# Layer-norm factors of an S4 and SwiGLU kernel: mean times scale factor on GpSimd in place of VectorE

## Chip, cores and metric

One core of a Trainium2 chip runs the whole program. The metric is the device time of one execution in microseconds (us). The program before was timed three times: median 1091.86 us, lowest 1090.23, highest 1092.86.

## What is computed

Two layers of the same pair of blocks work on `x` with 2048 rows of 512 features. In the reference:

```python
x = A_u
x = x + _A_ref(_layernorm(x, axis=-1), ...)   # S4: long convolution of each feature
x = x + _B_ref(_layernorm(x, axis=-1), ...)   # SwiGLU: (silu(x @ w_gate) * (x @ w_up)) @ w_down
x = x + _A_ref(_layernorm(x, axis=-1), ...)
x = x + _B_ref(_layernorm(x, axis=-1), ...)

def _layernorm(x, axis=-1, eps=1e-5):
    m = jnp.mean(x, axis=axis, keepdims=True)
    v = jnp.var(x, axis=axis, keepdims=True)
    return (x - m) / jnp.sqrt(v + eps)
```

The inner width of `_B_ref` is 1376. `_A_ref` builds a convolution kernel of 2048 taps for each of the 512 features from 128 complex modes and convolves along the rows.

## The kernel before

The rows are cut into four blocks of 512 rows (`T`, `NB`). Up to about 330 us the program builds the convolution kernels and their spectra, splits the weights into two fp16 halves, and does the first block's convolution; three norms of that part use another function, `stats`, which the diff does not touch. From then on it runs the steady part: for each pair of layer and block, in the order `SEQ = ((0, 0), (0, 1), (0, 2), (1, 0), (0, 3), (1, 1), (1, 2), (1, 3))`, the convolution of the next pair stands beside the feed-forward part of the present one.

- The convolution of a pair (`ssm_half`, two halves of 256 features). `inputs` loads the block into `n` (L238), `norm_x` normalises it in place (L255, four groups of 128 rows), `forward` splits it into two fp16 parts `z` (ScalarE L267, VectorE L232 in the helper `stt`) and transforms it on TensorE (L277); ScalarE (L278) and VectorE (L232, L285, L292) make spectra of it, and GpSimd stores them in DRAM (L739). VectorE multiplies spectra with those of the convolution kernel and adds up over earlier blocks (L812, L815; loads L808 and L810 on the SP queue), combines (L820, L821, L767, L768, L833 to L845), and the inverse transform runs on TensorE (L784) from an fp16 split `yl` (ScalarE L776, VectorE L232). The result is added into the block's rows (L793, or L232 with `pi`).
- The feed-forward part (`ffn`), twice per pair with 256 rows each. `ffn_norm` normalises two groups of 128 rows: L883 on ScalarE, then the fp16 split L884 (ScalarE) and L885 (VectorE), then the transposes L887 by DMA on the SP queue. `remainder` (L899 to L901, L906 to L913) takes the last 96 of the 1376 columns, the lines L930 to L939 the others: matrix products, silu on ScalarE (L936), product on VectorE (L937), fp16 split (ScalarE L938, VectorE L939). The product with `w_down` (L946 to L948) is added to the rows on VectorE (L953) and stored (L957).

Both norms of the steady part take their factors from `row_stats`, which is what the change edits. It returns `rs`, the reciprocal standard deviation, and `nb`, minus the mean times `rs`. Sums come from the accumulator of ScalarE's activation: L223 a scaled sum, L225 a sum of squares around the mean, L226 one operation on 2 or 4 columns that adds epsilon. GpSimd raises to the power -0.5 (L227), VectorE multiplies (L228), and ScalarE's L255 or L883 reads both as `scale` and `bias`. The feed-forward norms ask for `scale` = 256, the convolution's for 1.

`norm_x` runs 6 times (four columns) and `ffn_norm` 15 times (two columns); the first feed-forward half has its norm from the earlier part. The junk output of the sums goes to a scratch tile.

Each engine works through its own list in order. The lists of the early part are laid down by hand (`manual_schedule`). In the steady part a planner sets the order when the program is built: it replays the program with its own costs and due times (`schedule_with_timeline_sim=True`) and prefers what stands under `tc.high_priority(offset=BOOST)`, which holds for `ffn_norm`, the split lines of `ffn` and the transforms. An operation that waits for another engine holds up whatever stands behind it in its list.

Of the kernel before, what the change touches and what calls it, by code (L numbers as in the profile page):

```python
# [15 lines left out]
AF = mybir.ActivationFunctionType  # L16
OP = mybir.AluOpType
# [4 lines left out]
L, D, F = 2048, 512, 1376  # L22
# [53 lines left out]
def kernel(ctx, tc, x, a_re, a_im, b_re, b_im, c_re, c_im, log_dt, d_skip,  # L76
                           w_gate, w_up, w_down, c_ef, c_ei, c_ek, c_am, c_eh, c_eih, out):
    nc = tc.nc
    V, A, G, PE = nc.vector, nc.scalar, nc.gpsimd, nc.tensor
# [9 lines left out]
    def tl(shape, name, tag, dt=F32):  # L89
        return sb.tile(shape, dt, name=name, tag=tag, bufs=BUFS[tag])  # L90
# [50 lines left out]
    epst = sb.tile([P, 2], F32, name="epst")  # L141
# [74 lines left out]
    def row_stats(src, rows, scale, tag, junk):  # L216

        mv = tl([P, 4, 2], "mv", tag)
        rs = tl([P, 8], "rs", tag)
        nb = rs[:, 4:]  # L220
        c = 1.0 / (math.sqrt(D) * scale)
        for r in range(rows):
            A.activation(junk(r), src[:, r], AF.Identity, scale=-c / D, accum_out=mv[:, r, 0:1])  # L223
        for r in range(rows):
            A.activation(junk(r), src[:, r], AF.Square, scale=c, bias=mv[:, r, 0:1], accum_out=mv[:, r, 1:2])  # L225
        A.activation(mv[:, :rows, 1], mv[:, :rows, 1], AF.Identity, bias=epst[:, 0:1] if scale == 1.0 else epst[:, 1:2])  # L226
        G.tensor_tensor(rs[:, :rows], mv[:, :rows, 1], mhalf[:, :rows], OP.pow)  # L227
        V.scalar_tensor_tensor(nb[:, :rows], mv[:, :rows, 0], 1.0 / c, rs[:, :rows], OP.mult, OP.mult)  # L228
        return rs, nb

    def stt(o, i0, s, i1, op1):
# [20 lines left out]
    def norm_x(n):  # L252
        rs, nb = row_stats(n, 4, 1.0, "stats", lambda r: tl([P, D], "junk", "t1", BF16))
        for c in range(4):
            A.activation(n[:, c], n[:, c], AF.Identity, scale=rs[:, c:c + 1], bias=nb[:, c:c + 1])  # L255
# [618 lines left out]
    def ffn_norm(layer, b, s):  # L874

        rows = TB // P
        xt = xs[SEQ.index((layer, b)) % 3][:, s * rows:(s + 1) * rows]
        nh, nlo = nhl2[:, s % 2, 0], nhl2[:, s % 2, 1]
        with tc.high_priority(offset=BOOST):
            rs, nb = row_stats(xt, rows, 256.0, "stats2", lambda r: nn2[:, r])  # L880
            nt = nn2[:, 1].bitcast(F16).rearrange("p (i k) -> p i k", i=2)
            for r in range(rows):
                A.activation(nn2[:, 0], xt[:, r], AF.Identity, scale=rs[:, r:r + 1], bias=nb[:, r:r + 1])  # L883
                A.activation(nt[:, 0], nn2[:, 0], AF.Copy)  # L884
                V.tensor_tensor(nt[:, 1], nn2[:, 0], nt[:, 0], OP.subtract)  # L885
                for i, o in enumerate((nh, nlo)):
                    nc.sync.dma_start_transpose(o[:, :, r * P:(r + 1) * P], nt[:, i])  # L887
        return nh, nlo
# [86 lines left out]
    with tc.manual_schedule(engines={mybir.EngineType.Activation, mybir.EngineType.DVE, mybir.EngineType.PE, mybir.EngineType.Pool}):  # L975
# [170 lines left out]
        c, kts = NCH - 1, (kt2[:, 0], kt2[:, 1])  # L1146
# [160 lines left out]
```

## Time and profile before

| | |
|---|---|
| median of three runs | 1091.86 us |
| the profiled execution, time | 1091.58 us |
| the profiled execution, span from first to last instruction | 1089.4 us |
| granted TensorE clock, mean | 0.986 |
| busy: TensorE, VectorE, ScalarE, GpSimd | 1026.5, 969.3, 547.4, 109.6 us |

In the rows of the trace PE is TensorE (PEld its weight loads), DVE VectorE, ACT ScalarE, POOL GpSimd, and SP the queue that issues most transfers; a `q` behind an engine's name is its sequencer. L227 is line 227 of the program. A row of the timeline begins with start and duration in us, then engine, line, operation, written and read tiles, shapes and count; in brackets stands the idle time of the engine in front of it and what ended it. A row of the waits has the waiting operation, the one it waited for, the total in us, the number of times, and the longest. Matrix operations are pipelined and their ends are modelled; spans on GpSimd are rough.

### The profile page before, as it was taken

To read this page: it belongs to the slowest core of one execution; us is meant where nothing else is said; L and a number is where in the kernel's file an instruction comes from. 1 tells how busy PE (TensorE), PEld (TensorE's weight loads), DVE (VectorE), ACT (ScalarE), POOL (GpSimd) and SP (SyncE) were. 2 spreads that over 40 slices of the span, in tenths; PEclk is the share of its full clock that TensorE was granted. 3 is DMA by queue.
4 is the path that set the end of the run, shared out by engine and by line. 5 is a ranking of instruction groups with operands and counts; after the bars stand their busy time and mean duration, and the time that the engine had idled before them with its cause. 6 is when DMAs were issued, how large, how long until landed. Compare 5 with 4: busy or idle time off the path is not lost.

```text
span 1089.4 us, 22811 instructions
## 1 busy us (share of the span) xinstructions
PE 1026.5 (94%) x9302; PEld 810.9 (74%) x9302; DVE 969.3 (89%) x1405; ACT 547.4 (50%) x1093; POOL 109.6 (10%) x163
## 2 busy tenths in 40 slices
PE   1989999998779999999999999999999999999998
PEld 1868888887677777686779676786867687686775
DVE  8999999998999999999999989999998999993221
ACT  6989998953367162466462253533425432134211
POOL 1112222220002010012010001201100000000000
PEclk9989999998989999999999999999999999999999
DMA  5366777768765356342444553443545245312000
GB/s 212 108 180 167 173 166 179 187 181 272 234 182 172 120 145 215 105 141 68 131 117 133 158 160 130 119 136 100 166 126 180 59 127 147 109 61 63 2 25 20
DMA packets 125003, 149.23 MB, mean 137 GB/s; under 512 B 50897, under 2 KB 75985, under 8 KB 124130
## 3 DMA queue, kind: packets, MB, share of 16 engines
q1 hardware_dynamic: 112994, 122.27, 36.8%
q0 software_dynamic: 11904, 25.50, 10.0%
q8 instruction: 73, 1.20, 0.5%
q14 instruction: 32, 0.26, 0.1%
HBM read 97.66 MB, written 33.82 MB: 121 GB/s over the span
## 4 chain that ended last, share of the span: by engine, by line
PE 27%; DVE 27%; issue 11%; DMA 5%; ACT 3%; POOL 1%; SPq 0%; DVEq 0%; POOLq 0%; ACTq 0%
PE pgu L930 5%; PE pgu L931 5%; PE pgu L933 5%; DVE t L812 4%; DVE yk L815 4%; PE py L948 3%; PE py L946 3%; PE py L947 3%; DVE yk L812 3%; PE pi L784 2%; DVE sg L937 2%; DVE hl L939 2%; DMA n<-xdr 1%; DVE yl L232 1%; DMA mix<-nn 1%
## 5 line engine op out<-in xcount | busy, mean ns | idle before, releaser
L930 PE MATMUL pgu<-mix,wsl 128*128 128x256 f16 x1280 | 298.6, 273 | 5.4 <-DVE sg L937 2.1
L931 PE MATMUL pgu<-mix,wsl 128*128 128x256 f16 x1280 | 298.4, 273 | 0.0
L933 PE MATMUL pgu<-mix,wsl 128*128 128x256 f16 x1280 | 194.8, 273 | 0.0
L931 PEld LDWEIGHTS <-wsl 128*128 128x128 f16 x1280 | 125.2, 98 | 22.5 <-issue 6.7
L933 PEld LDWEIGHTS <-wsl 128*128 128x128 f16 x1280 | 125.2, 98 | 18.4 <-issue 3.8
L930 PEld LDWEIGHTS <-wsl 128*128 128x128 f16 x1280 | 125.2, 98 | 16.4 <-issue 1.2
L946 PE MATMUL py<-wsl,hh 128*128 128x512 f16 (+1 forms) x352 | 134.2, 381 | 0.1
L948 PE MATMUL py<-wsl,hl 128*128 128x512 f16 (+1 forms) x352 | 133.5, 381 | 0.1
L947 PE MATMUL py<-wsl,hh 128*128 128x512 f16 x320 | 121.8, 381 | 0.0
L815 DVE TENSOR_TENSOR yk<-yk,t 128x1024 f32<-128x1024 f32 x96 | 116.9, 1218 | 0.5
L812 DVE TENSOR_TENSOR t<-uu,w 128x1024 f32<-128x1024 f32 x96 | 117.0, 1218 | 0.3
L938 ACT ACTIVATE hh<-sg 128x512 f16<-128x512 f32 x80 | 50.1, 627 | 114.0 <-DVE sg L937 114.0
L544 PE MATMUL pw<-kt,ek 128*128 128x256 f32 (+1 forms) x384 | 93.2, 381 | 0.0
L937 DVE SCALAR_TENSOR_TENSOR sg<-pgu,sc,sg 128x512 f32<-128x512 f32 x80 | 59.6, 745 | 37.7 <-ACT sg L936 37.6
L936 ACT ACTIVATE sg<-pgu,sc 128x512 f32<-128x512 f32 x80 | 54.2, 678 | 70.7 <-PE pgu L933 66.9
L544 PEld LDWEIGHTS pw<-kt,ek 128*128 128x128 f32 x384 | 74.8, 199 | 8.8
L939 DVE TENSOR_TENSOR hl<-sg,hh 128x512 f16<-128x512 f32 x80 | 54.8, 685 | 15.3 <-ACT hh L938 15.3
L227 POOL TENSOR_TENSOR rs<-mv,mhalf 128x2 f32<-128x2 f32 (+1 forms) x21 | 33.6, 1598 | 336.3 <-ACT mv L226 296.3
L509 PE MATMUL pk<-re,g 128*32 128x64 f32 x1024 | 65.0, 317 | 2.2 <-DMA g<-g 1.9
L948 PEld LDWEIGHTS <-hl 128*128 128x128 f16 (+1 forms) x352 | 34.4, 98 | 39.2 <-issue 0.8
L947 PEld LDWEIGHTS <-hh 128*128 128x128 f16 (+1 forms) x352 | 34.6, 98 | 38.4 <-issue 0.8
L510 PE MATMUL pk<-im,g 128*32 128x64 f32 x1024 | 63.1, 301 | 0.0
(265 smaller groups left out, 2010.1 us busy)
## 6 DMA issues: line engine op xcount, KB each, us to landing
uu<-udr SPq DMA_DIRECT2D x96, 256.0 KB, 3.0
w<-wdr SPq DMA_DIRECT2D x96, 256.0 KB, 2.8
g<-g POOLq DMA_DIRECT2D x6, 1024.0 KB, 9.2
udr<-fu POOLq DMA_DIRECT2D x22, 256.0 KB, 2.7
udr<-u SPq DMA_DIRECT2D x16, 256.0 KB, 3.3
n<-xdr SPq DMA_DIRECT2D x4, 1024.0 KB, 6.4
kdr<-ks SPq DMA_DIRECT2D x6, 512.0 KB, 2.9
kt<-kdr SPq DMA_DIRECT2D x24, 128.0 KB, 3.0
```

Source lines behind the costliest of these rows:

```text
L509: PE.matmul(o, lhsT=g[:, 0, :, d], rhs=re[:, 0:64, d], start=True, stop=False, tile_position=(0, 32 * grp))
L544: PE.matmul(pw[:, i], lhsT=e, rhs=kt[:, :, c + 4 * k0:4 * k1:4, :].rearrange("p g k d -> p k g d"), start=c == 0, stop=c == 3)
L812: V.tensor_tensor(t, uu.unsqueeze(2).to_broadcast([P, NQ, 2, 2, DC]), w.unsqueeze(3).to_broadcast([P, NQ, 2, 2, DC]), OP.mult)
L815: V.tensor_tensor(yk, yk, t, OP.add)
L930: PE.matmul(o, lhsT=wgu(wi, k, 0)[:, fs], rhs=nh[:, k], start=k == 0, stop=False)
L931: PE.matmul(o, lhsT=wgu(wi, k, 1)[:, fs], rhs=nh[:, k], start=False, stop=False)
L933: PE.matmul(o, lhsT=wgu(wi, k, 0)[:, fs], rhs=nlo[:, k], start=False, stop=k == 3)
L937: V.scalar_tensor_tensor(sg, pgu[:, 1], sc6[:, 4:5], sg, OP.mult, OP.mult)
L939: V.tensor_tensor(hl[:, f0:f0 + 2], sg, hh[:, f0:f0 + 2], OP.subtract)
L946: PE.matmul(py[r], lhsT=hh[:n, f, rc], rhs=wd(f, 0)[:n], start=f == 0, stop=False)
L947: PE.matmul(py[r], lhsT=hh[:n, f, rc], rhs=wd(f, 1)[:n], start=False, stop=False)
L948: PE.matmul(py[r], lhsT=hl[:n, f, rc], rhs=wd(f, 0)[:n], start=False, stop=f == FT - 1)
```

## The change

The sums are no longer scaled: L223 yields minus the mean itself, L225 the plain sum of squares around it, and the constant 1 / (512 x scale^2) moves into L226. With the mean unscaled, its product with `rs` needs no constant, so it is a plain product of two small tiles, and it is issued on GpSimd behind the power instead of on VectorE. ScalarE's readers then wait for GpSimd instead of VectorE. `stats` stays as it is.

```diff
         mv = tl([P, 4, 2], "mv", tag)
         rs = tl([P, 8], "rs", tag)
         nb = rs[:, 4:]
-        c = 1.0 / (math.sqrt(D) * scale)
+        c = 1.0 / (D * scale ** 2)
         for r in range(rows):
-            A.activation(junk(r), src[:, r], AF.Identity, scale=-c / D, accum_out=mv[:, r, 0:1])
+            A.activation(junk(r), src[:, r], AF.Identity, scale=-1.0 / D, accum_out=mv[:, r, 0:1])
         for r in range(rows):
-            A.activation(junk(r), src[:, r], AF.Square, scale=c, bias=mv[:, r, 0:1], accum_out=mv[:, r, 1:2])
-        A.activation(mv[:, :rows, 1], mv[:, :rows, 1], AF.Identity, bias=epst[:, 0:1] if scale == 1.0 else epst[:, 1:2])
+            A.activation(junk(r), src[:, r], AF.Square, bias=mv[:, r, 0:1], accum_out=mv[:, r, 1:2])
+        A.activation(mv[:, :rows, 1], mv[:, :rows, 1], AF.Identity, scale=c,
+                     bias=epst[:, 0:1] if scale == 1.0 else epst[:, 1:2])
         G.tensor_tensor(rs[:, :rows], mv[:, :rows, 1], mhalf[:, :rows], OP.pow)
-        V.scalar_tensor_tensor(nb[:, :rows], mv[:, :rows, 0], 1.0 / c, rs[:, :rows], OP.mult, OP.mult)
+        G.tensor_tensor(nb[:, :rows], mv[:, :rows, 0], rs[:, :rows], OP.mult)
         return rs, nb
```

## Prediction

> **What bounds the kernel now.** First the page: busy time, and the chain that ended last.
>
> ```profile
> span 1089.4 us, 22811 instructions
> PE 1026.5 (94%) x9302; PEld 810.9 (74%) x9302; DVE 969.3 (89%) x1405; ACT 547.4 (50%) x1093; POOL 109.6 (10%) x163
> ...
> PE 27%; DVE 27%; issue 11%; DMA 5%; ACT 3%; POOL 1%; SPq 0%; DVEq 0%; POOLq 0%; ACTq 0%
> ```
>
> TensorE and VectorE share the chain; GpSimd is idle nine tenths of the time but still holds 1% of the chain. The changed function first runs at 331 us. Second, the windows view, for the stage in which VectorE still convolves and for the one in which only feed-forward work is left.
>
> ```profile
> 330.00:870.00 540.00, 527.51 (x4404) 401.19 (x4402) 521.90 (x786) 245.22 (x481) 51.60 (x62) 1.00 0.45 133
> 900.00:1060.00 160.00, 160.00 (x1347) 120.93 (x1346) 98.66 (x140) 43.13 (x77) 2.00 (x5) 1.00 0.24 68
> ```
>
> Columns: length, then busy time of PE, weight load, DVE, ACT, POOL. From 900 on TensorE has no idle time: nothing saved there on another engine can count. Between 330 and 870 TensorE is idle 540 - 527.5 = 12.5 us and VectorE 540 - 521.9 = 18.1 us. So 12.5 us is the most that a change of the norms can win, and ScalarE, busy 45%, matters only where something queued on it is late. Third, the waits of 330 to 870, VectorE's and then TensorE's.
>
> ```profile
> DVE hl L939 <- ACT hh L938: 7.0, 4, 3.0
> DVE rs L228 <- POOL rs L227: 5.0, 8, 1.2
> ...
> PE pi L784 <- ACT yl L776: 5.8, 4, 2.0
> PE pf L277 <- ACT fbt L278: 2.5, 1, 2.5
> PE pgu L930 <- DVE sg L937: 2.1, 2, 1.6
> PE pf L277 <- ACT z L267: 1.0, 1, 1.0
> ```
>
> VectorE stands 5.0 us behind the power (L227), in front of the operation that goes away (L228). But TensorE's own waits are mostly for ScalarE (5.8 + 2.5 + 1.0), only 2.1 for VectorE directly.
>
> **The change part by part.** The two sums (L223, L225) and the line after them (L226) keep their count, shape and engine; only constants move, so I cost them at nothing. If a constant did have a price it would fall on ScalarE, whose 45% leave room for it, and only the L226 in front of each power would pass it on. What is left is one operation fewer on VectorE and one more on GpSimd, 21 times.
>
> ```profile
> L227 POOL TENSOR_TENSOR rs<-mv,mhalf x21: 695/1269/4438, 331.2 to 993.8; 128x2 f32<-128x2 f32 x15, 128x4 f32<-128x4 f32 x6
> L228 DVE SCALAR_TENSOR_TENSOR rs<-mv,rs x21: 143/160/165, 334.4 to 994.6; 128x2 f32<-128x2 f32 x15, 128x4 f32<-128x4 f32 x6
> ...
> 441.67 0.17 DVE L228 SCALAR_TENSOR_TENSOR rs<-mv,rs 128x4 f32<-128x4 f32 x1 [0.26 <-POOL rs L227]
> 570.97 0.16 DVE L228 SCALAR_TENSOR_TENSOR rs<-mv,rs 128x2 f32<-128x2 f32 x1 [1.18 <-POOL rs L227]
> 703.42 0.16 DVE L228 SCALAR_TENSOR_TENSOR rs<-mv,rs 128x2 f32<-128x2 f32 x1 [0.60 <-POOL rs L227]
> 762.76 0.16 DVE L228 SCALAR_TENSOR_TENSOR rs<-mv,rs 128x2 f32<-128x2 f32 x1 [0.61 <-POOL rs L227]
> 832.93 0.16 DVE L228 SCALAR_TENSOR_TENSOR rs<-mv,rs 128x4 f32<-128x4 f32 x1 [0.54 <-POOL rs L227]
> 859.76 0.16 DVE L228 SCALAR_TENSOR_TENSOR rs<-mv,rs 128x2 f32<-128x2 f32 x1 [0.59 <-POOL rs L227]
> ```
>
> Removed on VectorE: 18 of the 21 lie before 870. Each holds the engine for about 0.11 us (the last row starts at 859.76, its follower, below, at 859.87): 18 x 0.11 = 2.0 us. With the 5.0 us of waits VectorE gets back 7.0 us. The six waits shown add up to 3.8 us; in the chain it is VectorE that goes on after each, so 3.8 + 6 x 0.11 = 4.4 us is the part that looks critical.
>
> Added on GpSimd: what one operation costs depends on what VectorE does. Rows of the power:
>
> ```profile
> 570.24 0.69 POOL L227 TENSOR_TENSOR rs<-mv,mhalf 128x2 f32<-128x2 f32 x1 [13.14 <-ACT mv L226]
> 831.87 1.02 POOL L227 TENSOR_TENSOR rs<-mv,mhalf 128x4 f32<-128x4 f32 x1 [33.72 <-ACT mv L226]
> 857.42 2.31 POOL L227 TENSOR_TENSOR rs<-mv,mhalf 128x2 f32<-128x2 f32 x1 [9.85 <-ACT mv L226]
> ...
> 857.95 1.22 DVE L815 TENSOR_TENSOR yk<-yk,t 128x1024 f32<-128x1024 f32 x1
> ...
> 859.87 1.23 DVE L812 TENSOR_TENSOR t<-uu,w 128x1024 f32<-128x1024 f32 x1
> 861.02 0.74 DVE L232 SCALAR_TENSOR_TENSOR xg<-pi,sy,xg 128x512 f32<-128x512 f32 x1
> 861.68 1.22 DVE L815 TENSOR_TENSOR yk<-yk,t 128x1024 f32<-128x1024 f32 x1
> 862.81 0.68 DVE L885 TENSOR_TENSOR nn<-nn 128x512 f16<-128x512 f32 x1
> ...
> L516 POOL TENSOR_TENSOR kt<-kt,tdk 1x64 f32<-1x64 f32 x1 | 0.6, 553 | 16.7 <-ACT kt L538 16.7
> ```
>
> With VectorE idle two columns take 0.69; four take 1.02 beneath an operation that reads one operand from PSUM. So a column of the power costs (1.02 - 0.69) / 2 = 0.165 and the fixed part is 0.69 - 0.33 = 0.36. The same 128x2 power took 2.31 at 857.42: VectorE's L815, with both operands in SBUF, ran until 859.17, VectorE then stood still for 0.59, and the power ended at 859.73, 0.56 after L815. So GpSimd is kept out while VectorE reads two SBUF operands, and here it was the very wait that now goes which let it in. SBUF — State Buffer (the Trainium skill, section "SBUF: two separate sides") says it more strictly: of a GpSimd operation that reads SBUF and a VectorE operation with two SBUF inputs, the first to start holds the shared ports for its whole length and "the other fully blocks". By that rule alone the case at 857 below costs its full 2.5 us and the sum comes to 1093.0 in place of 1092.5; this trace agrees at 857.42, but not to the letter at 482.21.
>
> There a power got in at the change between two such operations:
>
> ```profile
> 482.21 1.25 POOL L227 TENSOR_TENSOR rs<-mv,mhalf 128x4 f32<-128x4 f32 x1 [6.63 <-ACT mv L226]
> ...
> 481.34 1.22 DVE L812 TENSOR_TENSOR yk<-fu,w0r 128x1024 f32<-128x1024 f32 x1
> 482.48 0.68 DVE L939 TENSOR_TENSOR hl<-sg,hh 128x512 f16<-128x512 f32 x1
> ```
>
> It ended at 483.46, only 0.3 after L939 and 0.9 after L812, as if it had read when L812 ended at 482.56. So a changeover can let it in, and I count on that about one time in four.
>
> Price of the second operation, unhindered: not below 0.36 (the fixed part), not above 0.69 (a power); I take 0.45, between the two and below the 64-column addition of 0.55. It replaces 0.20 on the way to ScalarE (power done at 832.89, L228 done at 833.09). So every factor comes 0.25 us later even at best: bounds +0.16 and +0.49. Hindered, it adds what VectorE still has to run until its next operation with a PSUM operand.
>
> Who waits for that: L883 or four L255 on ScalarE, and in its queue behind them the casts L938, the silu L936 and the copies L776, L278 that VectorE and TensorE need. On GpSimd the stores of spectra (L739) and the memset L906 come later by as much as the second operation takes; their readers are the loads L810 of a later block and the transposes L913 behind two more operations on VectorE and ScalarE, which cover the 0.5 us and not a delay of several, so I cost them at nothing and leave the rest to the range. On SP the transposes L887 of a late norm hold the loads L808 and L810 queued behind them, which VectorE's L812 reads.
>
> Now the two places near the end of the stage. **857 us.** What follows on ScalarE and TensorE:
>
> ```profile
> 859.96 0.81 ACT L883 ACTIVATE nn<-xg,rs 128x512 f32<-128x512 f32 x1 [2.62 <-DVE rs L228]
> ...
> 867.15 0.63 ACT L884 ACTIVATE nn<-nn 128x512 f16<-128x512 f32 x1 [2.81 <-DMA mix<-nn]
> 867.69 0.58 ACT L278 ACTIVATE fbt<-pf 128x512 f32<-128x512 f32 x1
> ...
> 868.32 0.81 PE L277 MATMUL pf<-z,eh 128*128 128x256 f16 x6 [2.50 <-ACT fbt L278]
> ```
>
> TensorE's 2.50 us at 868.32 is its last wait of the program, and it hangs on this norm: L278 stands behind the second L884, that behind the transposes of the first row, those behind L883. Without L228, L812 starts at 859.2 and ends at about 860.4; the power gets in there and is done at 860.4 + 0.56, about 860.95; the second operation misses L232 (over at 861.0), waits for L815 until 862.2 and is done near 862.5: L883 starts 2.5 later. If the changeover at 859.2 lets the power in, the second one runs beneath L232 and L883 starts 0.7 later. I take +2.0.
>
> **831 us.** The four-row norm of the last block:
>
> ```profile
> 833.13 2.93 ACT L255 ACTIVATE n<-n,rs 128x512 f32<-128x512 f32 x4
> ...
> 836.54 1.04 ACT L267 ACTIVATE z<-n 128x1024 f16<-128x1024 f32 x1
> ...
> 837.63 0.38 PE L277 MATMUL pf<-z,eh 128*128 128x256 f16 x2 [0.99 <-ACT z L267]
> ...
> 838.46 0.74 DVE L937 SCALAR_TENSOR_TENSOR sg<-pgu,sc,sg 128x512 f32<-128x512 f32 x1
> 839.12 1.21 DVE L232 SCALAR_TENSOR_TENSOR z<-n,z 128x1024 f16<-128x1024 f32 x1
> ```
>
> The power runs as now. The second operation would start at 832.9 under an L812 that now begins at 832.4, and get in at 833.5 at the earliest, near 837.8 (L937) at the latest: the factor comes 0.6 to 4.9 later. VectorE needs L267's result, ready at 837.58, at 839.12, a slack of 1.5. I take 2.0 late, 0.5 beyond the slack, which VectorE's 0.54 + 0.11 won there pays back: zero.
>
> **Upstream of 812 us** VectorE wins 0.26 + 1.18 + 0.60 + 0.61 and 15 slots of 0.11: 4.3 us. Since 5.8 us of TensorE's waits are for ScalarE's yl (L776), which stands behind the norms' own sums and not behind L228, I pass on half: -2.1. Against it ScalarE is late in 16 norms by 0.25 to some us; I take 1.0 lost.
>
> Sum: -2.1 + 1.0 + 0 + 2.0 = +0.9 us. The profiled execution took 1091.58 us (span 1089.4 and 2.2 around it), 0.3 below the median of 1091.86, so 1091.6 + 0.9 = 1092.5.
>
> **The rivals.** *Faster: VectorE is the bound.* All six waits lie on the chain, and TensorE has 12.5 us of idle time to give. If the second operation slips in at changeovers, the 4.4 us come through, and 857 costs 0.7: 1091.6 - 4.4 + 0.7 = 1087.9. For it: chain and waits name the power; against it: TensorE waits for ScalarE. It decides if L883 starts within 0.7 us of its old distance to the power's start.
>
> *Slower: the second operation is shut out, and ScalarE's queue stands.* One mechanism: VectorE runs on until it needs a cast queued behind the waiting L883; only then does GpSimd get in, and VectorE stands for 0.36 + 0.81 + 0.63 = 1.8 us, three times its old wait of 0.6. At five norms of 18 that is 9.0 us; less the 7.0 that VectorE gained, plus 2.5 at 857: 1091.6 + 4.5 = 1096.1. For it: the 2.31 row, and the largest power of 4.44 us (4438 ns in the row of L227). Against it: at 859.96 ScalarE waited 2.62 and VectorE ran on. It decides from three such norms on.
>
> *Nothing happens:* TensorE's work alone sets the end, and both effects lie beside it: 1091.6, in the same band as my sum.
>
> **How the numbers follow.** A measurement of this kernel tells about 0.2% (2.2 us) from no change. My sum and "nothing happens" together 0.35; faster 0.32; slower 0.33. The planner that orders the instructions also sees another program and may swap neighbours; that has no row and goes to both sides. Range: down to the faster case less 3 (the other 2.6 us of VectorE's 7.0), 1085; up to the slower case plus two more such norms, 3.6 us, rounded up, 1100. My own case alone: 1090 to 1094.5.
>
> **What would show it.** Right: L228 gone, GpSimd's second operation 0.4 to 0.7 long where VectorE is idle and over 1 us elsewhere; VectorE's 5.0 us of waits gone but its waits for L938 above 7.0; L883 near 857 some 2 us later after its power; TensorE's last wait still by L278 and longer. Wrong: second operations under 0.5 us throughout (then faster), or new TensorE waits behind 870, where I have none.

## The result, and the profile after

The changed kernel takes 1105.68 us in the median (1102.05 to 1107.73), the kernel before beside it 1091.38: ratio 1.0126, interval 1.0109 to 1.0142. It is 14.3 us slower, outside the range that was forecast. The profiled execution took 1106.34 us, its span is 1104.5. In after's rows every line from 227 on is one higher than before: the power is L228, the new GpSimd product L229, the first ScalarE reader of a feed-forward norm L884, the splits L885 and L886.

The page of after (span, busy times, then the shares of the chain) and the windows view (length, then busy PE, weight load, DVE, ACT, POOL):

```profile
span 1104.5 us, 22812 instructions
PE 1030.5 (93%) x9302; PEld 813.9 (74%) x9302; DVE 968.6 (88%) x1384; ACT 545.9 (49%) x1093; POOL 129.8 (12%) x184
...
PE 47%; DVE 23%; DMA 12%; ACT 8%; issue 6%; POOL 3%; SPq 1%; DVEq 0%; ACTq 0%; POOLq 0%
```

```profile
330.00:870.00 540.00, 517.53 (x4305) 393.89 (x4304) 512.88 (x757) 240.70 (x474) 67.05 (x78) 1.00 0.44 132
870.00:900.00 30.00, 27.93 (x249) 22.44 (x248) 24.22 (x33) 12.96 (x27) 4.59 (x4) 0.94 0.48 113
900.00:1060.00 160.00, 159.96 (x1325) 118.78 (x1324) 109.62 (x151) 43.88 (x78) 2.60 (x8) 1.00 0.26 78
```

VectorE is busy 0.7 us less than before and TensorE 4.0 us more, 2.4 of them ahead of the first changed norm; the other 11.1 of the 15.1 us by which the span is longer are idle time of TensorE. From 330 to 870 TensorE now stands 540 - 517.5 = 22.5 us where it stood 12.5, VectorE 27.1 where it stood 18.1. Another 2.1 us of TensorE's idle time lie in 870 to 900. The first changed norm's power starts at 334.07 in place of 331.24: 2.8 us of this one execution come from ahead of the change, where nothing was edited.

The waits of after, 330 to 870, VectorE's and then TensorE's (total, times, longest):

```profile
DVE hl L940 <- ACT hh L939: 9.1, 6, 3.2
DVE nn L886 <- ACT nn L885: 6.6, 5, 1.6
DVE nn L886 <- DMA mix<-nn: 4.2, 5, 1.3
DVE sg L938 <- ACT sg L937: 3.4, 4, 1.1
```

```profile
PE pgu L931 <- DVE sg L938: 5.6, 5, 1.7
PE pf L278 <- ACT z L268: 3.3, 2, 1.7
PE pi L785 <- ACT yl L777: 3.3, 4, 1.7
PE pgu L931 <- DVE sg L909: 2.6, 3, 1.0
```

VectorE's 5.0 us behind the power are gone. In their place it stands 10.8 us in front of the split of the norm (L886), where it had stood 1.3, and 9.1 instead of 7.0 at L940. TensorE, which had waited mostly for ScalarE, waits first for VectorE's products (L938, L909). The two operations on GpSimd, as groups (count, then shortest, median and longest in ns), and who waited for the second:

```profile
L228 POOL TENSOR_TENSOR rs<-mv,mhalf x21: 695/1033/3254, 334.1 to 1008.5; 128x2 f32<-128x2 f32 x15, 128x4 f32<-128x4 f32 x6
...
L229 POOL TENSOR_TENSOR rs<-mv,rs x21: 195/682/6829, 336.9 to 1009.3; 128x2 f32<-128x2 f32 x15, 128x4 f32<-128x4 f32 x6
...
  ACT nn L884: 32.8, 13
  ACT n L256: 10.3, 5
```

The product is shorter than any bound of mine when nothing is in its way (0.195 us) and up to 6.8 us when something is. That looked like the whole story, but a second thing differs. Compared instruction by instruction, the lists of the two programs are the same up to 331 us; behind that 133 of VectorE's instructions and 71 of ScalarE's stand elsewhere. The planner, which sets each engine's list when the program is built, laid out the steady part anew.

### The profile page after: what moved, and what is told of

Same layout as the page of the kernel before. It is cut to its first block, busy times and chain, and to the rows that moved or that the text cites. A ratio compares the mean times of both kernels' runs of the same rounds, so it can differ in the third digit from the quotient of the medians.

```text
span 1104.5 us, 22812 instructions
## 1 busy us (share of the span) xinstructions
PE 1030.5 (93%) x9302; PEld 813.9 (74%) x9302; DVE 968.6 (88%) x1384; ACT 545.9 (49%) x1093; POOL 129.8 (12%) x184
## 4 chain that ended last, share of the span: by engine, by line
PE 47%; DVE 23%; DMA 12%; ACT 8%; issue 6%; POOL 3%; SPq 1%; DVEq 0%; ACTq 0%; POOLq 0%
PE pgu L931 6%; PE pgu L932 6%; PE pgu L934 6%; PE pw L545 5%; PE py L949 4%; PE py L948 4%; PE py L947 4%; DVE t L813 3%; DMA mix<-nn 3%; PE pk L510 3%; DMA g<-g 3%; PE pi L785 2%; DVE yk L816 2%; PE pk L511 2%; DVE yk L813 2%
## 5 line engine op out<-in xcount | busy, mean ns | idle before, releaser
L931 PE MATMUL pgu<-mix,wsl 128*128 128x256 f16 x1280 | 300.2, 273 | 12.8 <-DVE sg L938 5.6
L932 PEld LDWEIGHTS <-wsl 128*128 128x128 f16 x1280 | 125.5, 98 | 30.8 <-issue 15.1
L939 ACT ACTIVATE hh<-sg 128x512 f16<-128x512 f32 x80 | 49.9, 624 | 95.4 <-DVE sg L938 95.3
L938 DVE SCALAR_TENSOR_TENSOR sg<-pgu,sc,sg 128x512 f32<-128x512 f32 x80 | 59.5, 743 | 37.0 <-ACT sg L937 36.9
L940 DVE TENSOR_TENSOR hl<-sg,hh 128x512 f16<-128x512 f32 x80 | 54.7, 684 | 17.8 <-ACT hh L939 17.6
L228 POOL TENSOR_TENSOR rs<-mv,mhalf 128x2 f32<-128x2 f32 (+1 forms) x21 | 27.5, 1309 | 342.3 <-ACT mv L226 342.3
L947 PEld LDWEIGHTS <-hh 128*128 128x128 f16 (+1 forms) x352 | 34.4, 98 | 39.5 <-ACT hh L939 1.8
L948 PEld LDWEIGHTS <-hh 128*128 128x128 f16 (+1 forms) x352 | 34.4, 98 | 39.1 <-issue 2.0
```

The source lines that it names most:

```text
L931: PE.matmul(o, lhsT=wgu(wi, k, 0)[:, fs], rhs=nh[:, k], start=k == 0, stop=False)
L932: PE.matmul(o, lhsT=wgu(wi, k, 1)[:, fs], rhs=nh[:, k], start=False, stop=False)
L938: V.scalar_tensor_tensor(sg, pgu[:, 1], sc6[:, 4:5], sg, OP.mult, OP.mult)
L947: PE.matmul(py[r], lhsT=hh[:n, f, rc], rhs=wd(f, 0)[:n], start=f == 0, stop=False)
L948: PE.matmul(py[r], lhsT=hh[:n, f, rc], rhs=wd(f, 1)[:n], start=False, stop=False)
```

## The experiments

Two theories were set against each other first: *shut out* (GpSimd's two operations wait for VectorE, ScalarE's queue stands) and *order* (the planner's new order is worse, whoever multiplies). To part them, the order of each engine is pinned: instructions are chained in a given list, with no semaphore added. `_ORDER` holds the lists of the old or of the new program.

```diff
+    info = mybir.DependencyInfo(mybir.DependencyClass.NoSync, mybir.DependencyReason.DATA)
+    for engine, packed in _ORDER.items():
...
+        for a, b in zip(names, names[1:]):
+            tc.add_manual_dep(made[b], made[a].name, info, reason="order")
```

Line numbers of a pinned kernel are 2 higher than in the kernel before, some 1 or 2 more. The cuts of code show the operations alone; calls that only mark an added or missing instruction for the lists are left out. Ratios are to the kernel before, timed beside each run, and a difference given in us is the ratio's; the medians themselves can differ from it by a microsecond.

**1. Changed operations, old order.** The diff of the change, with the lists of before.

> The changed program, each engine's instructions pinned to the order they had before the change; only the GpSimd product, its inputs and the missing VectorE instruction differ from the kernel before. Theory 'shut out' (the product and the power on GpSimd wait for VectorE, ScalarE's queue stands, its followers come late): 1103 to 1106 us, as the changed kernel; in the trace second products of 1 to 7 us and VectorE standing at L886 behind ScalarE. Theory 'order' (the planner, given other costs, put 133 VectorE and 71 ScalarE instructions elsewhere, and that order is worse): 1090 to 1093 us, with the second products just as long now and then. Between them, say 1097, each has a share.

1094.39 us, ratio 1.0025 (1.0008 to 1.0041): +2.7 us.

**2. Old operations, new order.** The kernel before with the lists of after.

> The kernel before (product on VectorE, scaled mean), each engine's instructions pinned to the order that the changed kernel has. Theory 'shut out': 1090 to 1093 us, since no second GpSimd operation exists to be shut out; VectorE's waits for the power at the product are back (about 5 us from 330 us on). Theory 'order': 1103 to 1107 us, with TensorE's stalls spread over the stage from 330 to 870 us as in the changed kernel.

1101.24 us, ratio 1.0088 (1.0061 to 1.0116): +9.6 us. So both theories hold a part, and the order has most of it: 2.7 + 9.6 = 12.3 of 13.8 (1.0126), the rest within the intervals. Both times *order* came nearest and missed its range, by 1.4 and 1.8 us, because it stood for one cause alone.

**3. No product, old order.** The cut is against the kernel before; the sums are written as in the change, as in run 4. The norm's shift stays unmultiplied.

```diff
-        nb = rs[:, 4:]
+        nb = mv[:, :, 0]
...
-        V.scalar_tensor_tensor(nb[:, :rows], mv[:, :rows, 0], 1.0 / c, rs[:, :rows], OP.mult, OP.mult)
```

> Pinned to the order of the kernel before, with no product at all: ScalarE takes minus the mean, unmultiplied, as its bias, so the norm's shift is left out of the computation; one GpSimd operation is left, the power. It bounds what any place for the product can win. Both theories: VectorE's 5.0 us of waits at the product go and nothing is put in their place. My sum on record gives 1091.6 - 4.4 + 1.0 = 1088 us; if VectorE's waits are only swapped for later ones, 1091 us. If it is slower than 1093, the wait at the product did something useful (it held VectorE off the power), and that is a third theory: 'unheld VectorE', by which VectorE's standing at the product was what let GpSimd's power in; then the powers (L228) grow from their time of before.

1086.31 us, ratio 0.9946 (0.9923 to 0.9969): -5.9 us. That is what taking the product off every engine is worth: VectorE's wait and operation go, and ScalarE gets its factors without the 0.2 us of the product. The run does not part the two.

**4. Product on ScalarE, old order.**

```diff
-        V.scalar_tensor_tensor(nb[:, :rows], mv[:, :rows, 0], 1.0 / c, rs[:, :rows], OP.mult, OP.mult)
+        for r in range(rows):
+            A.activation(nb[:, r:r + 1], mv[:, r, 0:1], AF.Copy, scale=rs[:, r:r + 1])
```

> Pinned to the order of the kernel before; the product is made on ScalarE, row by row right before its readers, so neither VectorE nor GpSimd has a second step. 84 small ScalarE instructions more (four for a norm of four rows), an estimated 0.2 us each, or 0.8 us a norm on ScalarE's queue. Theory 'shut out': faster than the changed kernel by most of its loss, 1089 to 1095 us, since ScalarE needs only the power. Theory 'order': the same, 1089 to 1095. Theory 'unheld VectorE': 1098 us or more, because here too VectorE no longer stands while GpSimd raises to the power.

1088.54 us, ratio 0.9968 (0.9946 to 0.9989): faster than both kernels. *Unheld VectorE* is out. There are 54 such instructions, not the 84 of the expectation, and they took 0.28 us each.

**Which norm carries the 2.7 us?** In the old order with GpSimd's product, the norm at 331 us stands out. Timeline (start, duration, engine; in brackets the idle time in front), GpSimd, then rows of VectorE, then ScalarE's reader:

```profile
331.91 2.72 POOL L229 TENSOR_TENSOR rs<-mv,mhalf 128x4 f32<-128x4 f32 x1 [39.48 <-ACT mv L228]
334.71 7.43 POOL L230 TENSOR_TENSOR rs<-mv,rs 128x4 f32<-128x4 f32 x1
...
333.74 0.73 DVE L939 SCALAR_TENSOR_TENSOR sg<-pgu,sc,sg 128x512 f32<-128x512 f32 x1
334.40 0.40 DVE L838 TENSOR_TENSOR bb<-bb 128x256 f32<-128x256 f32 x1
...
341.40 0.67 DVE L941 TENSOR_TENSOR hl<-sg,hh 128x512 f16<-128x512 f32 x1
342.00 0.67 DVE L795 TENSOR_TENSOR xg<-xg,pi 128x512 f32<-128x512 f32 x1
...
342.17 2.93 ACT L257 ACTIVATE n<-n,rs 128x512 f32<-128x512 f32 x4 [4.59 <-POOL rs L230]
```

The power gets through under L939, which reads PSUM (`pgu`). The product then waits while 13 VectorE operations begin one after the other, all on tiles in SBUF, and ends 0.14 us after L795 (`pi` in PSUM) began; ScalarE stands 4.59 us. In the kernel before, VectorE made this product in 0.14 us and ScalarE read it without a wait:

```profile
334.40 0.14 DVE L228 SCALAR_TENSOR_TENSOR rs<-mv,rs 128x4 f32<-128x4 f32 x1
...
337.94 2.92 ACT L255 ACTIVATE n<-n,rs 128x512 f32<-128x512 f32 x4
```

Two kernels move it back, all in the old order: **5.** all six convolution norms on VectorE, **6.** only this one.

```diff
-        G.tensor_tensor(nb[:, :rows], mv[:, :rows, 0], rs[:, :rows], OP.mult)
+        (V if scale == 1.0 else G).tensor_tensor(nb[:, :rows], mv[:, :rows, 0], rs[:, :rows], OP.mult)   # 5
+        (G if seen else V).tensor_tensor(nb[:, :rows], mv[:, :rows, 0], rs[:, :rows], OP.mult)           # 6
```

> The changed program in the order of the kernel before, but the six convolution norms have their product on VectorE; only the 15 feed-forward norms have it on GpSimd. With all 21 on GpSimd it was 1094.4 against 1091.2. My steps put the price at feed-forward norms and nothing at the convolution norms: then 1093 to 1095 us. If the long second operations of the convolution norms (7.4 us at 335 us) carry it: 1090 to 1092 us.

> The changed program in the order of the kernel before (1094.4 us), but for one norm of 21: the convolution norm at 331 us has its product on VectorE again. There the GpSimd product took 7.4 us, from 334.7 to 342.1, and ScalarE stood 4.6 us for it. Theory 'one norm' (what the GpSimd product itself costs is lost there): 1090.5 to 1092.5 us. Theory 'five other convolution norms, or all': 1093 to 1095 us.

1090.96 us, ratio 0.9993 (0.9978 to 1.0009), and 1091.79 us, ratio 0.9997 (0.9983 to 1.0011). The expectation that the feed-forward norms carry the price is refuted. One norm of 21 seems to make the 2.7 us, though the intervals of runs 1 and 6 overlap a little. With it on VectorE the other 20 GpSimd products come out level with the VectorE ones: by the difference to run 3, what their removal from VectorE wins is lost again behind GpSimd. In the order of before, then, the change could have been had for nothing, though not with a gain.

**Where in the order is the loss?** In run 2 the longest stall of TensorE is at 651.74, and it can be followed back. Rows of ScalarE, VectorE and TensorE:

```profile
645.85 0.63 ACT L225 ACTIVATE junk<-n 128x512 bf16<-128x512 f32 x1 [8.32 <-DMA n<-xdr]
...
648.35 0.69 DVE L941 TENSOR_TENSOR hl<-sg,hh 128x512 f16<-128x512 f32 x1 [5.92 <-ACT hh L940]
...
651.74 0.27 PE L932 MATMUL pgu<-mix,wsl 128*128 128x256 f16 x1 [4.62 <-DVE sg L939]
```

ScalarE stands 8.32 us in front of a norm's sums for a late block; a cast (L940) whose input is there stands behind three of them; VectorE waits for the cast and TensorE for VectorE. **7, 8.** The new order up to about 600 us only, and from there only. **9.** The whole new order with that cast put in front of the sums.

In words, ScalarE's list changes so:

```diff
-ACT: ..., sum, sum, sum, hh, sum, ...
+ACT: ..., hh, sum, sum, sum, sum, ...
```

> The kernel before (product on VectorE); what it does up to about 600 us is pinned to the order of the changed kernel, the rest to the order of the kernel before. The whole new order with the same operations cost 9.6 us (1101.2 against 1091.6 on record, 1091.2 beside it). Theory 'one place' (most of it is lost where ScalarE stands 8.3 us on a late block load near 640 us, VectorE behind it 5.9 us and TensorE 4.6 us): 1091 to 1094 us here. Theory 'spread' (many small losses in all of the stage): 1095 to 1097 us.

> The reverse: the order of the kernel before up to about 600 us, then that of the changed kernel; operations of the kernel before. 'One place': 1098 to 1101 us, with TensorE's stall of 4 to 5 us near 645 us. 'Spread': 1095 to 1097 us. If both halves together give much less than 9.6 us, it is the seam or the combination, and neither holds.

> The kernel before in the whole new order, but for one ScalarE instruction: the fp16 split that stands behind three of the four sums of the norm near 645 us (where ScalarE waits for the block's load) is put in front of them. 'One place': TensorE's 4.6 us at that point go and do not come back: 1096 to 1097.5 us against 1101.2. 'Spread', with slack taken up later: 1099 to 1101 us.

Ratios 1.0043 (1.0024 to 1.0062), 1.0042 (1.0023 to 1.0061) and 1.0076 (1.0048 to 1.0104). The halves share the loss and add up (0.85% against 0.88%); the move's gain cannot be told from none. *One place* falls.

**Is it any new order?** **10.** The product on ScalarE, laid out by the planner. **11, 12.** Useless VectorE copies in front of the feed-forward norms' products, in the old order and in the planner's.

```diff
+        if rows == 2:
+            V.tensor_copy(rs[:, 3:4], rs[:, 1:2])
         V.scalar_tensor_tensor(nb[:, :rows], mv[:, :rows, 0], 1.0 / c, rs[:, :rows], OP.mult, OP.mult)
```

> The product on ScalarE as before (1088.5 us in the pinned order), but the planner lays out the order itself; it moves 182 VectorE and 85 ScalarE instructions against the pinned one. Theory 'draw' (each edit of the norm makes the planner lay out the steady part anew, and the order of the kernel before is better than what it comes to otherwise): 1095 to 1103 us. Theory 'GpSimd only' (the planner's order suffers because it prices the GpSimd product wrongly, other edits are harmless): 1087 to 1091 us.

> Nothing of the change is in it: the kernel before, with one useless VectorE copy of 128 x 1 in front of each of the 15 feed-forward norms' products, pinned to the order of the kernel before. Price of the copies themselves, 15 of an estimated 0.1 us, at most 1.5 us: 1091 to 1093.5 us under every theory. It is the control of the next run.

> The same 15 useless copies, but the planner lays out the order itself; with them it moves 177 VectorE and 72 ScalarE instructions against the kernel before. Theory 'draw' (any edit that shifts the planner's times makes another order, and the order of the kernel before is an unusually good one): 1097 to 1106 us. Theory 'norm edits' (the order gets worse only where ScalarE's readers hang on GpSimd or ScalarE instead of VectorE): 1090 to 1094 us.

Run 10: 1104.21 us, 1.2 us above the range of *draw*, ratio 1.0123 (1.0082 to 1.0164), 1.6% behind its own pinned run. Run 11: 1.0002 (0.9983 to 1.0020), so pinning itself costs nothing that shows. Run 12: 1093.94 us, 1.0017 (1.0003 to 1.0030), though it moves more instructions than the change does. *Draw* falls in its strong form: orders differ, and something makes some of them bad. Run 12 lies in the range of *norm edits*, by which ScalarE's readers must hang on GpSimd or ScalarE for a bad order; runs 16 and 17 below bear on that.

**13, 14. One kind of instruction.** In the two bad orders, of the changed kernel and of run 10, VectorE's splits of the norm (L885 of before) stand 1.87 places earlier on average, in the mild one half a place later. Run 13 moves only these 30 in the old order, run 14 puts them back in the new one. Only these 30 entries of VectorE's list move, as far as no engine then waits in a circle: 62 places earlier in sum in run 13 (the new order has 56), and back to all but 12 in run 14.

> The kernel before in its old order, except that VectorE's 30 splits of the feed-forward norms (L885 of the kernel before) stand where the new order has them: 62 places earlier in sum, about two each, and up to 9 (the new order: 56). Nothing else is moved. Theory 'split early' (the planner, with no product on VectorE, believes the norm ready sooner, puts the split ahead of work that is ready, and VectorE stands for ScalarE): 1096 to 1101 us, with VectorE's waits at the split up from 1.3 us to 6 or more. Theory 'many kinds' (the loss is the sum of all the moves, the split being one of many): 1091 to 1094 us.

> The reverse: the whole new order with the operations of the kernel before (1101.2 us), but the splits put back to where the old order has them, as far as the rest allows (12 places early in sum are left of 56). 'Split early': 1092 to 1096 us. 'Many kinds': 1098 to 1102 us.

Run 13: 1105.12 us, 4 us above its range, ratio 1.0117 (1.0089 to 1.0145). That single kind costs 12.8 us; its waits of VectorE and TensorE, 330 to 870:

```profile
DVE nn L887 <- ACT nn L886: 10.3, 8, 2.0
DVE nn L887 <- DMA mix<-nn: 6.5, 4, 4.6
DVE hl L941 <- ACT hh L940: 3.8, 4, 1.3
```

```profile
PE pi L786 <- ACT yl L778: 7.1, 6, 1.9
PE pgu L932 <- DVE sg L939: 5.4, 3, 3.1
```

VectorE stands 16.8 us at the splits (L887 here), as the theory said. But run 14, which should have been better than run 2, is worse: 1108.48 us, 1.0153 (1.0133 to 1.0174), above both its ranges, with 12.5 us of VectorE's waits now at the cast's reader:

```profile
DVE hl L941 <- ACT hh L940: 12.5, 8, 4.9
DVE sg L939 <- ACT sg L938: 8.8, 10, 1.5
```

So an early split is enough for a loss of this size, but it is not shown to be the loss of the new order: moving this one kind alone spoils either order. It seems that the lists fit each other; which part of the new order costs its 9.6 us stays open.

**15 to 17. The missing operation.** Run 15 is run 3 (no product), laid out by the planner. Runs 16 and 17 leave the order to the planner too, with the product on GpSimd and on ScalarE, but give VectorE a useless product that waits for the power; it goes to spare columns of the tile `epst`.

```diff
+        V.scalar_tensor_tensor(epst[:, 2:2 + rows], mv[:, :rows, 0], 1.0, rs[:, :rows], OP.mult, OP.mult)
         G.tensor_tensor(nb[:, :rows], mv[:, :rows, 0], rs[:, :rows], OP.mult)    # 16; 17: on ScalarE, row by row
```

> No product at all, as in the pinned run of 1086.3 us (ScalarE takes minus the mean unmultiplied, so the norm's shift is left out of the computation), but the planner lays out the order; 150 VectorE and 87 ScalarE instructions move. Theory 'missing product' (the planner's order is worse whenever VectorE has no product in its list, as with the product on ScalarE, 16 us worse): 1095 to 1103 us. Theory 'chance' (orders scatter, as with the useless copies, 2 to 3 us worse): 1086 to 1092 us.

> The changed kernel (GpSimd's product feeds ScalarE) with a useless product on VectorE as well, which waits for the power as the old one did and which nothing reads; the planner lays out the order, and moves 221 VectorE and 125 ScalarE instructions against the kernel before, more than in the changed kernel (133 and 71). Theory 'missing product' (without an operation in VectorE's list that waits for the power the planner's order is bad): 1093 to 1097 us, that is the price of the GpSimd product (2.7) and a mild reshuffle. Theory 'chance' (how bad an order is has nothing to do with that operation): anywhere up to 1110, and above 1099 it refutes the first.

> The same with the product on ScalarE and a useless VectorE product that waits for the power; the planner lays out the order, and moves 217 VectorE and 104 ScalarE instructions. Without the useless product it was 1104.2 in the planner's order and 1088.5 in the old one. 'Missing product': 1089 to 1094 us. 'Chance': above 1097.

Run 15: 1104.14 us, 1.0104 (1.0071 to 1.0137). Run 16: 1098.51 us, 1.0051 (1.0032 to 1.0071). Run 17: 1096.37 us, 1.0031 (1.0012 to 1.0050). All three lie 1.1 to 2.4 us above the range of *missing product*; *chance* is missed by 12 us in run 15 and not reached in run 17, and run 16 refutes neither. The kernel before ran at 1093.45 beside the last two, so ratios are compared:

| what VectorE has behind the power | product | old order | planner's order | order's share |
|---|---|---|---|---|
| nothing | GpSimd | 1.0025 | 1.0126 | 1.0% |
| nothing | ScalarE | 0.9968 | 1.0123 | 1.6% |
| nothing | none | 0.9946 | 1.0104 | 1.6% |
| the product, and copies | VectorE | 1.0002 | 1.0017 | 0.2% |
| a useless product | GpSimd | not run | 1.0051 | 0.3% over 1.0025 (without it) |
| a useless product | ScalarE | not run | 1.0031 | 0.6% over 0.9968 (without it) |

A useless operation makes the changed kernel 0.7% faster and the ScalarE version 0.9%. Three layouts without a VectorE operation that waits for the power lose 1.0 to 1.6%, three with one 0.2 to 0.6%. That is shown for these six layouts. In the last two rows part of the 0.3 and 0.6% may be the wait that the useless product itself brings, which no run in the old order prices. *Norm edits* does not fit: in runs 16 and 17 the readers hang on GpSimd and ScalarE, and the loss is small.

Three things stay open. How the planner comes from the one to the other is in no trace. No run has an operation on VectorE that does not wait for the power, so it may be any added operation that helps. And the place of the split does not sort the layouts: counted in the traces, it stands 2.7 places earlier on average in run 15, but most splits of runs 16 and 17 stand earlier too, while a few norms' splits moved back by 57 to 88 places.

**18. Last, a faster version.** Run 4 with the cast of run 9 moved as there.

> Candidate for a faster version: product on ScalarE in the order of the kernel before (1088.5 us), and the one move that gained 1.4 us in the new order (the fp16 split in front of the sums of the norm near 640 us, where ScalarE waits 5.5 us for a load). Theory 'local stalls last': 1086 to 1087.5 us. 'Slack takes them up': 1088 to 1089.5 us.

1087.13 us, ratio 0.9967 (0.9938 to 0.9995), no better than run 4 by any measure here. Both are 0.3% faster than the kernel before, and 1.6% faster than the changed one.

## Why the prediction was wrong

- **The step that failed**: "The planner that orders the instructions also sees another program and may swap neighbours; that has no row and goes to both sides." A term put at nothing is the largest one, +9.6 us by run 2, and it is not symmetric: none of the planner's six new layouts is shown to be faster than the old order, and the three without VectorE's operation are slower by 1.0 to 1.6%. No row of the profile of before could have priced it; but the program's source told that a planner fixes the lists, and VectorE's operation stood in one of them.
- **Removed on VectorE.** The 7.0 us given back, 4.4 of them critical, were halved to -2.1 because TensorE's waits name ScalarE. Run 3 gives -5.9 (-8.4 to -3.4), with ScalarE's 0.2 us a norm in it: the chain's 4.4 lies inside the interval, the halved 2.1 does not.
- **Added on GpSimd.** The price unhindered, "not below 0.36", was 0.195: the fixed part of a power is not that of a product behind it. Hindered, the rule held for most: of the 14 products of run 1 that took over 0.21 us, 9 ended as VectorE began to read PSUM or stood still, and 5 at a change between two operations on SBUF. The 1.0 for "16 norms" and 2.0 for 857 us should have been 5.9 + 2.7 = 8.6 (run 1 against run 3). That +0.9 was forecast for the operations and +2.7 measured is luck: two errors, -3.8 and +5.6, cancel for the most part.
- **857 us.** Not +2.0. In run 1 and in after ScalarE stands 3.17 us there in place of 2.62: the product slipped in beneath an operation with a PSUM operand, the case I had priced at 0.7. **831 us**: the product took 0.6 us and the reader came 0.5 us later, by which zero is plausible, though no run prices this norm alone. The norm that counted, as far as runs 5 and 6 tell, is the one at 331 us, in the sum of "16 norms", where its cover was the ScalarE time until 337.9 and the product came at 342.1.
- **The slower rival.** Its mechanism is there: in after VectorE stands 1.6 us in front of the split at four norms (from 409.6, 581.8, 694.9 and 714.6) and 0.9 at 874.3. Its sum of +4.5 us was too large for the operations alone (+2.7, and that from the norm at 331 us) and too small for the change.
- **What would show it.** VectorE's waits for ScalarE's cast above 7.0: yes, 9.1. TensorE's last wait by L278 and longer: no. It is this row, behind 870, which I had named as a sign of being wrong:

```profile
PE pgu L931 <- DVE sg L909: 2.1, 1, 2.1
```

## What to carry to other kernels

When a planner fixes the order, time an edit twice: in its own layout and with the lists pinned to the old one; here the operations cost 0.25% and the layout 0.9%. An operation that makes an engine wait may be what keeps a layout good, and whether to remove it is a question for both runs. Here the price of a small operation on GpSimd came from the one norm where VectorE's run of operations on SBUF was long (7.43 us), so ask for that norm and not for the mean.

## What the runs showed of the hardware

The product took 0.195 to 0.201 us in the free cases, with two columns and with four, against 0.695 for a power on two columns. In the stretch quoted above 13 VectorE operations began while the product waited, and at none of these changeovers did it get in; I had counted on one in four. SBUF — State Buffer (the Trainium skill, section "SBUF: two separate sides") gives the ports to whichever of the two started first, for its whole length; this stretch agrees with it over 7.43 us, if VectorE takes them again at each of its starts. Over all 21 norms of run 1, 21 such changeovers kept a waiting product out and 5 let it in (at 391.3, 488.1, 560.5, 650.8 and 839.2), which is near the one in four; what sets the 5 apart is not shown.
